# Which weights and values stay on chip, in which places, and in which pieces the query weights come

## The chip, the cores and the metric

The kernel runs on one core of a Trainium2 chip. The core has five engines that run side by side: TensorE (PE, matrix products, with its weight loads PEld), VectorE (DVE), ScalarE (ACT), GpSimd (POOL) and SyncE (SP), which here only issues DMA transfers. Transfers bring data from HBM to the on-chip memory SBUF; TensorE writes its results to PSUM, which has eight banks. The metric is the device time in microseconds (us) of one execution; lower is better.

## The reference

Two rounds of attention and a gated feed-forward block (GLU) for 4 batch rows with one new token each. Both rounds use the same caches and weights.

```python
def _A_ref(x, k_cache, v_cache, wq, wo):
    W = min(4096, max(256, Sk // 4))          # 2048 of 8192 positions
    q = (x @ wq).reshape(B, Sq, Hq, Dh)...    # 32 query heads of 128
    k = jnp.repeat(k_cache[:, :, Sk - W:, :], rep, axis=1)   # 8 key heads, rep = 4
    v = jnp.repeat(v_cache[:, :, Sk - W:, :], rep, axis=1)
    p = softmax(q k^T * Dh ** -0.5)
    return (p v).reshape(B, Sq, Hq * Dh) @ wo
def _B_ref(x, w_gate, w_up, w_down):          # 512 -> 1792 -> 512
    return (sigmoid(x @ w_gate) * (x @ w_up)) @ w_down
x = x + _A_ref(_layernorm(x), ...)
x = x + _B_ref(_layernorm(x), ...)
x = x + _A_ref(_layernorm(x), ...)
x = x + _B_ref(_layernorm(x), ...)
```

All inputs are bf16. The keys of the window are 16 MB, the values 16 MB, the query weights 4 MB, the output weights 4 MB, and gate, up and down weights 1.75 MB each.

## The kernel before

**Order of the work.** The kernel records every operation with its reads, writes and PSUM banks in a list; a planner (`_schedule`) then orders the list for each engine by estimated times, and `_assign_sync` adds the waits on semaphores. All transfers but one go through SP, in the order in which they are recorded. A transfer waits until the place that it fills has been read for the last time, and everything behind it on SP waits with it. Line L464 is the one line that issues them.

**Layers.** The code counts four layers: 0 is attention, 1 the GLU, 2 attention again, 3 the GLU again. In layer 0 each of 8 heads loads its keys (2 MB), turns them with TensorE (L740) and keeps the turned keys in `kt` for layer 2. Scores are made at L763, the softmax maximum at L772 to L782, the exponential at L785, the weights are turned at L796 and spread at L821 (VectorE) and L828 (ScalarE). Values are loaded (`load_v`, 2 MB a head) and multiplied at L863 or L921; where several blocks are summed in one product, ScalarE copies the partial sums at L872 and TensorE adds them at L879. The output weights are applied at L988 or L946 and L895. In layer 2 the keys are there already, and values, and the weights that are not kept, are loaded again.

**Places.** SBUF is cut into units of 256 columns, 64 KB over all 128 partitions. `ar` is an arena of 75 units, `sx` a side area of 31, `ws` the output weights' place (64 units), `kt` the keys' place (256), `pt`, `pb` and `qs` small buffers. A dictionary `WHERE` says which units a load fills, and `blk_tok` turns units into tokens through which the planner finds who must have read them. Between layers 0 and 2 the output weights of five blocks of `ws` are moved aside into PSUM banks (`stash`, L1036) and brought back by ScalarE (L1031), so that their units can hold feed-forward and query weights.

**What is kept before.** Rows 0 and 1 of gate and up (`u01`, `g01`, 28 units) are loaded in layer 1 and used again in layer 3. Of the values, 8 units of head 0 and 13 units of head 7 stay from layer 0 to layer 2 (`VKEEP` names the piece that `load_v` leaves out). Together these are 49 units. Half of the query weights stays too (`WKEEP`); the other half (32 units) is streamed again for layer 2, as three pieces listed in `WHERE["q01"]`.

**The stretch around the change.** After the last head of layer 0, layer 1's weights come: up rows 0 and 1, gate rows 0 and 1, gate rows 2 and 3, up rows 2 and 3, then the down weights in six pieces. `glu` runs its products at L1157 in the order up 0, up 1, gate 0 to 3, up 2, up 3, and the down products at L1233 (L1230 in layer 3). Then the streamed query weights, then values for layer 2. `project_q` multiplies the query weights (L703), takes the mean off (L716) and scales by the reciprocal deviation (L719), which GpSimd makes at L634; heads 0 to 3 and 4 to 7 of the keys have a half of `qs` each (tokens `qs` and `qs1`). The first scores of layer 2 wait for the first half alone, the later ones for both. `scores` alternates between the PSUM banks in `SB2 = [3, 0]`; the bank `MB` (4) takes a part of the turned weights later. A memset of `qs` by GpSimd (L1318) runs before the queries are written, because a weight piece has lain there.

## Time and profile before

| | us |
|---|---|
| median of 3 runs (lowest, highest) | 174.04 (173.87, 174.45) |
| the profiled execution | 174.79 |
| its span, first to last instruction | 173.0 |
| TensorE busy | 136.2 |
| VectorE busy | 100.7 |
| ScalarE busy | 77.3 |
| transfers, moved | 68.93 MB, 398 GB/s over the span |

The profiled execution is one of its own and not among the three of the median. In the profile a line such as `L863 PE MATMUL ps<-kt,pt` is an operation of TensorE at line 863 that writes `ps` and reads `kt` and `pt`; what stands in brackets is the time that its engine sat idle before and who ended it. `SPq` is the issue of a transfer, and the time of landing is given apart. The granted TensorE clock (PEclk) is a share of full speed.

### The profile page before, as it was taken

How to read it: one execution, taken by the hardware profiler on the slowest of the kernel's cores; microseconds unless marked ns; L12 is line 12 of the kernel's file. 1: busy time of each engine (PE TensorE's matmuls, PEld its weight loads, DVE VectorE, ACT ScalarE, POOL GpSimd, SP SyncE). 2: the span in 40 equal slices, each digit the busy share in tenths (PEclk: the TensorE clock that was granted, in tenths of full speed). 3: DMA queues.
4: the chain of work that ended last, by engine and by line, in shares of the span. 5: the costliest groups of instructions: out<-in, count | busy, mean ns of one | idle time of the engine just before them, and what ended most of it. 6: DMA issues, size and time to landing. Idle time of an engine off the chain costs nothing.

```text
span 173.0 us, 4894 instructions
## 1 busy us (share of the span) xinstructions
PE 136.2 (79%) x2179; PEld 100.4 (58%) x2179; DVE 100.7 (58%) x252; ACT 77.3 (45%) x134; POOL 8.0 (5%) x19
## 2 busy tenths in 40 slices
PE   0395589899898779998979676657977989689883
PEld 0292388658466458565655366546625756458772
DVE  7535015886848675795797653113279877754450
ACT  2064207848576646566291230110767463554200
POOL 5200000000000000000000000202200000000020
PEclk9999756999999987999999755555569999956755
DMA  5999999999999999999999999999999999999960
GB/s 183 424 422 411 432 424 428 439 409 449 424 416 433 400 445 424 412 427 428 420 417 418 397 419 416 406 400 411 386 385 452 426 420 405 424 416 423 407 250 5
DMA packets 9361, 68.93 MB, mean 398 GB/s; under 512 B 1017, under 2 KB 1917, under 8 KB 6013
## 3 DMA queue, kind: packets, MB, share of 16 engines
q1 hardware_dynamic: 9332, 68.62, 95.7%
q8 instruction: 17, 0.28, 0.6%
q14 instruction: 4, 0.02, 0.0%
q10 hardware_dynamic: 8, 0.00, 0.0%
HBM read 68.62 MB, written 0.00 MB: 397 GB/s over the span
## 4 chain that ended last, share of the span: by engine, by line
DMA 65%; PE 23%; DVE 6%; ACT 2%; issue 2%; SPq 1%; DVEq 0%; ACTq 0%
DMA arena<-in_A_v_cache_dram 32%; DMA kt<-in_A_k_cache_dram 12%; DMA kt<-in_A_v_cache_dram 10%; DMA wo_sb<-in_B_w_down_dram 7%; PE ps L863 5%; PE ps L740 4%; DMA wo_sb<-in_A_wq_dram 4%; PE ps L763 3%; PE ps L1157 2%; PE ps L921 2%; SPq L464 1%; DVE pt L821 1%; PE ps L1230 1%; PE ps L836 1%; PE ps L988 1%
## 5 line engine op out<-in xcount | busy, mean ns | idle before, releaser
L750 ACT COPY kt<-ps 128x1024 bf16<-128x1024 bf16 x40 | 39.2, 1017 | 28.2 <-PE ps L740 28.0
L740 PE MATMUL ps<-ident_r,kt 128*128 128x128 bf16 x512 | 40.4, 238 | 5.1 <-DMA kt<-in_A_k_cache_dram 3.1
L740 PEld LDWEIGHTS ps<-ident_r,kt 128*128 128x128 bf16 x512 | 34.9, 109 | 11.8 <-issue 4.4
L750 DVE COPY kt<-ps 128x1024 bf16<-128x1024 bf16 x24 | 29.1, 1214 | 14.2 <-PE ps L740 14.0
L763 PE MATMUL ps<-kt,qs 128*32 128x512 bf16 x256 | 18.3, 413 | 1.2 <-ACT pb L785 1.2
L821 DVE TENSOR_TENSOR pt<-ps,ofbr 128x1024 bf16<-128x1024 f32 (+1 forms) x15 | 15.4, 1029 | 2.7 <-PE ps L796 2.7
L863 PE MATMUL ps<-arena,pt 128*64 128x512 bf16 (+1 forms) x128 | 13.1, 377 | 3.0 <-DMA arena<-in_A_v_cache_dram 3.0
L772 DVE TENSOR_REDUCE nmz<-ps 128x1 f32<-128x512 f32 x16 | 11.0, 688 | 5.9 <-PE ps L763 5.8
L791 DVE STREAM_TRANSPOSE pb<-pb 128x512 bf16<-128x512 bf16 x16 | 11.3, 704 | 4.2 <-ACT pb L785 4.1
L785 ACT ACTIVATE pb<-ps,nmz 128x512 bf16<-128x512 f32 x16 | 11.1, 692 | 5.8 <-DVE nmz L782 5.8
L828 ACT ACTIVATE pt<-ps,ofbr 128x96 bf16<-128x96 f32 x28 | 7.2, 342 | 7.8 <-PE ps L796 7.8
L863 PEld LDWEIGHTS ps<-arena,pt 128*64 128x64 bf16 (+1 forms) x128 | 5.9, 111 | 7.9 <-DMA arena<-in_A_v_cache_dram 4.0
L763 PEld LDWEIGHTS ps<-kt,qs 128*32 128x32 bf16 x256 | 5.8, 101 | 7.8 <-ACT pb L785 2.2
L872 ACT COPY arena<-ps 128x512 f32<-128x512 f32 (+1 forms) x7 | 3.9, 555 | 11.9 <-PE ps L863 11.7
L1031 ACT COPY wo_sb<-ps 128x1024 bf16<-128x1024 bf16 x5 | 5.0, 1011 | 9.1 <-PE ps L703 9.1
L836 PE MATMUL ps<-rowf,nmz 128*128 128x16 f32 x32 | 6.9, 292 | 2.7 <-DVE pt L821 2.5
L836 PEld LDWEIGHTS ps<-rowf,nmz 128*128 128x128 f32 x32 | 5.4, 212 | 5.8 <-DVE pt L821 4.2
L1157 PE MATMUL ps<-xn,arena 128*128 128x5 bf16 (+1 forms) x168 | 6.3, 172 | 2.2 <-DMA arena<-in_B_w_up_dram 1.1
L634 POOL TENSOR_TENSOR rs<-pt,rs 128x4 f32<-128x4 f32 x3 | 3.0, 1014 | 106.0 <-DVE pt L630 106.0
L879 PEld LDWEIGHTS ps<-arena 128*128 128x128 f32 x52 | 6.7, 201 | 2.1 <-ACT arena L872 1.6
L879 PE MATMUL ps<-arena 128*128 128x16 f32 x52 | 7.4, 273 | 0.6
L1157 PEld LDWEIGHTS ps<-xn,arena 128*128 128x128 bf16 x168 | 6.3, 118 | 2.5 <-DMA arena<-in_B_w_up_dram 1.2
(170 smaller groups left out, 162.9 us busy)
## 6 DMA issues: line engine op xcount, KB each, us to landing
kt<-in_A_k_cache_dram SPq DMA_DIRECT2D x8, 2048.0 KB, 24.6
arena<-in_A_v_cache_dram SPq DMA_DIRECT2D x7, 2048.0 KB, 20.2
kt<-in_A_v_cache_dram SPq DMA_DIRECT2D x3, 2048.0 KB, 14.9
wo_sb<-in_A_wo_dram SPq DMA_DIRECT2D x8, 512.0 KB, 25.1
kt<-in_A_v_cache_dram SPq DMA_DIRECT2D x4, 1024.0 KB, 19.3
kt<-in_A_wq_dram SPq DMA_DIRECT2D x1, 2048.0 KB, 11.7
side<-in_A_wq_dram SPq DMA_DIRECT2D x1, 1984.0 KB, 15.8
arena<-in_B_w_up_dram SPq DMA_DIRECT2D x2, 896.0 KB, 8.0
```

What stands on the lines that cost most here:

```text
L740: last = pe.transpose(bankb(bank)[:, (v * NB + q) * 128:(v * NB + q + 1) * 128], kt[:, c0:c0 + 128], ident_b[:, :])
L750: return (e.tensor_copy if ev == "vector" else e.copy)(to, fr)
L763: last = pe.matmul(ps[32 * b:32 * b + 32, sbk, 0:CB * 128], qs[:, q0:q0 + 32], blk_ap(kblk(h, b))[:, c * CB * 128:(c + 1) * CB * 128], sta ...
L772: lambda v: v.tensor_reduce(nmv, ps[:, sbk, 0:CB * 128], AXX, ALU.max, negate=True),
L785: o = a.activation(pbuf[:, :], ps[:, sbk, 0:CB * 128], ACTF.Exp, bias=gv, scale=1.0, accum_out=zv)
L791: P.op("vector", "ptr%d_%d" % (L, h), 650.0, lambda v: v.transpose(turned[:, :], pbuf[:, :]), r=[("pb", 0), ("pb", 1)], w=[("pb", 2), ("pb ...
L821: lambda v: v.tensor_tensor(pv4[:, 0:nj], spread(tbk, nj).unsqueeze(2).broadcast_to([128, nj, NB, REP]), ofb[:, :].unsqueeze(1).unsqueeze( ...
L828: last = a.mul(pv4[:, nj:NJ4, b, :], spread(MB, NJ4 - nj), ofb[:, b:b + 1])
L836: lambda pe: pe.matmul(ps[:, tbk, CB * NQ:CB * NQ + NR], zv.broadcast_to([128, 128]), rowf[:, :], start=True, stop=True),
L863: last = pe.matmul(ps[rows * g:rows * (g + 1), bank, 0:wide * 128].rearrange("p (c d) -> p c d", c=wide), ptv[:, w0:w0 + rows], v, start=( ...
L879: last = pe.matmul(ps[:, out[0], out[1]:out[1] + NR], part[:, c * 128:(c + 1) * 128], ey[wide][:, c * NR:(c + 1) * NR], start=(c == 0), st ...
L1157: last = pe.matmul(ps[:, bank, fc * wid:(fc + 1) * wid], cols[:, fc - g0, :], xn[:, ktc * (NB + 1):ktc * (NB + 1) + wid], start=(ktc == 0 ...
```

## The change

**Kept.** Gate rows 0 are no longer kept; up rows 0 and 1 and gate rows 1 are (21 units). Of the values 24 units of head 0 and 15 of head 7 are kept. Together 60 units. In layer 3, gate rows 0 are loaded again (7 units, into `kt`, free by then).

**Places and pieces.** The kept weights and values change places, and the rest is fitted around them. In layer 1 up rows 2 and 3 come as 7 units, 4 units and 3 units, in `ar`, `pb` and `qs`; gate rows 2 and 3 come before 0 and 1. The down weights come in the order of blocks 4 to 5, 0 to 3, 8 to 11, 6 to 7, 12 to 13, partly in places that layer 1's own gate rows have just left. The streamed query weights come in five pieces of 8, 8, 8, 4 and 4 units instead of three of 10, 14 and 8, and not in row order: the first two hold both halves of the rows for the first sixteen query heads, which serve key heads 0 to 3. They go to places that layer 1's weights leave. Value head 0 of layer 2 needs one load instead of four.

**Scores.** The first scores of layer 2 are made in bank `MB` instead of bank 3.

**Order in the feed-forward.** A variable `turn` gives the order of the products: up 0, up 1, then gate 2, 3, 0, 1 in layer 1 and gate 1, 0, 2, 3 in layer 3, then up 2, up 3. Which product opens and closes an accumulation follows from it.

```diff
-    KEEPG = 4
+    KEPTG = {("u", 0), ("u", 1), ("g", 1)}
...
-    VKEEP = {0: 24, 7: 19}
+    VKEEP = {0: 8, 7: 17}
...
-        WHERE["V0_%d" % (HKV - 1)] = [ar(0, 19), ar(23, 13)]
-        WHERE["u01"], WHERE["g01"] = ar(52, 2 * GU), ar(38, 2 * GU)
+        WHERE["V0_%d" % (HKV - 1)] = [ar(15, 17), ar(0, 15)]
+        WHERE["u01"], WHERE["g01"] = ar(36, 2 * GU), ar(22, 2 * GU)
...
-            "g23_1": ("ws", 8, 2 * GU), "u23_1": ar(0, 2 * GU),
-            "d0_1": ar(14, 8), "d4_1": ("ws", 22, 6), "d7_1": ar(36, 2), "d8_1": ("qs", 0, 4), "d10_1": ("pb", 0, 4),
-            "d12_1": ("pt", 4, 4),
-            "q01": [("ws", 8, 10), ar(0, 14), ("ws", 18, 8)],
-            "V2_0": [ar(14, 9), ar(36, 2), sx(0, 8), sx(8, 5), ar(66, 8)],
-            "V2_1": [sx(13, NS - 13), ar(0, 14)],
+            "g23_1": ("ws", 8, 2 * GU), "u2_1": ar(15, GU), "u3_1": ("pb", 0, 4), "u3_1b": ("qs", 0, 3),
+            "d4_1": ("ws", 24, 4), "d6_1": ("pt", 4, 4), "d0_1": ("ws", 8, 8), "d8_1": ("ws", 16, 8), "d12_1": ar(25, 4),
+            "q01": [(0, ar(15, 8)), (16, ("ws", 8, 8)), (8, ("ws", 16, 8)), (24, ("ws", 24, 4)), (28, ar(25, 4))],
+            "V2_0": [sx(0, 8), ar(50, 24)],
+            "V2_1": [sx(8, NS - 8), ar(15, 9)],
             "V2_6": [("kt", 128, 16), ("kt", 144, 16)],
-            "V2_7": [("kt", 160, 12), ("kt", 172, 7), ar(23, 13)],
-            "g23_3": ar(0, 2 * GU), "u23_3": sx(0, 2 * GU),
-            "d0_3": ar(14, 8), "d4_3": ("kt", 192, 8), "d8_3": ("kt", 200, 8), "d12_3": sx(14, 4),
+            "V2_7": [("kt", 160, 10), ("kt", 170, 7), ar(0, 15)],
+            "g0_3": ("kt", 0, GU), "g23_3": ar(15, 2 * GU), "u23_3": sx(0, 2 * GU),
+            "d0_3": ("kt", 8, 8), "d4_3": ("kt", 192, 8), "d8_3": ("kt", 200, 8), "d12_3": sx(14, 4),
...
+        def qz(s):
+            return (("qs",), ("qs1",)) * (s[0] == "qs")
+
+        def load_g(L, nm, ktc):
+            kept = (nm, ktc) in KEPTG
+            name = "%s%d_%d" % (nm, ktc, L)
+            if not kept and name in WHERE:
+                got, f0 = [], 0
+                for x in (name, name + "b"):
+                    if x in WHERE:
+                        s, c0 = WHERE[x], ktc % 2 * F + f0 * 128
+                        dma("w" + x, blk_ap(s), (wg_d if nm == "g" else wu_d)[:, ktc // 2, c0:c0 + s[2] * UNIT], w=blk_tok(s) + qz(s),
+                            rate="bw_4k")
+                        got.append((s, f0))
+                        f0 += 2 * s[2]
+                return got
...
-            for nm, ktc in (("u", 0), ("u", 1), ("g", 0), ("g", 1), ("g", 2), ("g", 3), ("u", 2), ("u", 3)):
+            turn = [("u", 0), ("u", 1)] + [("g", a) for a in ((1, 0, 2, 3) if last_layer else (2, 3, 0, 1))] + [("u", 2), ("u", 3)]
+            for at, (nm, ktc) in enumerate(turn):
...
-                parts[1:] = [(4, 7), (7, 8), (8, 10), (10, 12), (12, 14)]
+                parts = [(4, 6), (0, 4), (8, 12), (6, 8), (12, 14)]
...
-        for w in WHERE["q01"]:
+        for u0, w in WHERE["q01"]:
...
-            turns.append(scores(2, n, h, SB2[n % 2], TB2[n % 2]))
+            turns.append(scores(2, n, h, SB2[n % 2] if n else MB, TB2[n % 2]))
```

In `VKEEP` the number is the unit at which the kept piece starts within the head, so `0: 8` means that head 0's units from 8 on are kept. In `q01` the number is the unit at which a piece starts; units 0 to 15 are the first rows of each pair of row blocks, 16 to 31 the second.

More of the change, by code (lines that the diff above doesn't have):

```diff
@@ L421, in build @@
         MAIN = WKEEP[2][0][1]
-        G0 = MAIN - KEEPG * GU
         def ar(u, n):
@@ L1040, in build @@
         gkeep = {}
-        def load_g(L, nm, ktc, keep):
-            key = (nm, ktc // 2, 0 if keep or (nm, ktc // 2, 0) in gkeep else L)
+        def qz(s):
[13 more added lines that the diff above has]
+                return got
+            key = "%s%d%d" % (nm, ktc // 2 * 2, ktc // 2 * 2 + 1) + ("" if ktc < 2 else "_%d" % L)
+            s = WHERE[key]
             if key not in gkeep:
-                s = WHERE["%s%d%d" % (nm, key[1] * 2, key[1] * 2 + 1) + ("_%d" % L if key[2] else "")]
                 gkeep[key] = s
-                dma("w%s%d_%d" % (nm, L, ktc), blk_ap(s), (wg_d if nm == "g" else wu_d)[:, key[1], :], w=blk_tok(s),
-                    rate="bw_7k")
-            s = gkeep[key]
-            return (s[0], s[1] + ktc % 2 * GU, GU)
+                dma("w" + key, blk_ap(s), (wg_d if nm == "g" else wu_d)[:, ktc // 2, :], w=blk_tok(s), rate="bw_7k")
+            return [((s[0], s[1] + ktc % 2 * GU, GU), 0)]
         def load_d(L, fc0, fc1):
@@ L1056, in load_d @@
             dma("wd%d_%d" % (L, fc0), blk_ap(s)[:, 0:(fc1 - fc0) * D], rows[:, (fc0 - g0) * D:(fc1 - g0) * D],
-                w=blk_tok(s) + (("qs",), ("qs1",)) * (s[0] == "qs"), rate="bw_4k")
+                w=blk_tok(s), rate="bw_4k")
             return s
@@ L1146, in glu, with e_g @@
             wid = NB if last_layer else NB + 1
-            for nm, ktc in (("u", 0), ("u", 1), ("g", 0), ("g", 1), ("g", 2), ("g", 3), ("u", 2), ("u", 3)):
+            turn = [("u", 0), ("u", 1)] + [("g", a) for a in ((1, 0, 2, 3) if last_layer else (2, 3, 0, 1))] + [("u", 2), ("u", 3)]
+            for at, (nm, ktc) in enumerate(turn):
                 bank = GB if nm == "g" else UB
-                keep = not last_layer and 2 * ktc + (nm == "u") < KEEPG
-                s = load_g(L, nm, ktc, keep)
-                def e_g(pe, ktc=ktc, s=s, bank=bank):
+                first, end = ktc == turn[0 if nm == "u" else 2][1], ktc == turn[-1 if nm == "u" else 5][1]
+                got = load_g(L, nm, ktc)
+                def e_g(pe, ktc=ktc, got=got, bank=bank, first=first, end=end):
                     last = None
@@ L1155, in e_g @@
                         g0, gn = WD[fc // 4]
-                        cols = blk_ap(s)[:, g0 * 128:(g0 + gn) * 128].rearrange("p (m j) -> p j m", j=gn)
+                        s, f0 = [x for x in got if x[1] <= fc][-1]
+                        cols = blk_ap(s)[:, (g0 - f0) * 128:(g0 - f0 + gn) * 128].rearrange("p (m j) -> p j m", j=gn)
                         last = pe.matmul(ps[:, bank, fc * wid:(fc + 1) * wid],
@@ L1159, in e_g @@
                                          xn[:, ktc * (NB + 1):ktc * (NB + 1) + wid],
-                                         start=(ktc == 0 and fc == 0), stop=(ktc == NC - 1),
-                                         skip_group_check=True)
+                                         start=(first and fc == 0), stop=end, skip_group_check=True)
                     return last
                 prev = [P.op("tensor", "glu_%s%d_%d" % (nm, L, ktc), 36.0 * NFC, e_g,
-                             r=list(blk_tok(s)) + [("xn",)], w=[("psg", bank, ktc)], banks=(bank,), order=prev)]
+                             r=[t for s, _ in got for t in blk_tok(s)] + [("xn",)], w=[("psg", bank, ktc)], banks=(bank,), order=prev)]
                 toks[nm].append(("psg", bank, ktc))
@@ L1233, in e_d @@
                                 last = pe.matmul(ps[:, YB, c * NB:(c + 1) * NB], wd, hf,
-                                                 start=(fc == 0 and c == 0), stop=(fc == NFC - 1),
+                                                 start=(fc == parts[0][0] and c == 0), stop=(fc == parts[-1][1] - 1),
                                                  skip_group_check=True)
@@ L1315, in build @@
         glu(1, False)
-        P.op("gpsimd", "qs_zero", 1200.0, lambda g: g.memset(qs[:], 0.0), w=[("qs",), ("qs1",)] + list(blk_tok(WHERE["d8_1"])))
+        P.op("gpsimd", "qs_zero", 1200.0, lambda g: g.memset(qs[:], 0.0), w=[("qs",), ("qs1",)] + list(blk_tok(WHERE["u3_1b"])))
         layer_norm(2, SCALE)
         streamed = []
-        u0 = 0
-        for w in WHERE["q01"]:
+        for u0, w in WHERE["q01"]:
             dma("wq2_%d" % u0, blk_ap(w), wq_d[:, 0, u0 * UNIT:(u0 + w[2]) * UNIT], w=blk_tok(w),
@@ L1329, in build @@
                     streamed.append((blk_ap(t), blk_tok(t), ktc, q0, q1))
-            u0 += w[2]
-        assert u0 == HQ
+        assert sum(w[2] for _, w in WHERE["q01"]) == HQ
         project_q(2, kept_q + streamed, 1)
```

## The prediction

> **What bounds the kernel now.** I read the page's slices and its chain of waits first, then the windows of busy time, the DMA issues of the stretch 98 to 132 us with their time to landing, and the timeline around the places the change touches.
>
> ```profile
> GB/s 183 424 422 411 432 424 428 439 409 449 424 416 433 400 445 424 412 427 428 420 417 418 397 419 416 406 400 411 386 385 452 426 420 405 424 416 423 407 250 5
> DMA 65%; PE 23%; DVE 6%; ACT 2%; issue 2%; SPq 1%; DVEq 0%; ACTq 0%
> ```
>
> The transfers run near 420 GB/s in every slice but the first and the last two, and 65% of the chain is transfers. So bytes count, as long as nobody lets the queue run dry.
>
> ```profile
> core 0: us, PE busy (x) PEld busy (x) DVE busy (x) ACT busy (x) POOL busy (x), PEclk, DMA share, GB/s
> 98.90:112.40 13.50, 9.42 (x191) 8.05 (x190) 4.77 (x17) 2.96 (x5) 1.01 (x1) 0.50 1.01 414
> 118.40:123.40 5.00, 4.30 (x125) 4.01 (x125) 2.16 (x12) 1.09 (x2) 1.35 (x3) 0.50 1.01 395
> 123.40:127.10 3.70, 3.64 (x48) 1.60 (x48) 1.85 (x6) 2.86 (x3) 0.00 (x0) 0.50 1.01 378
> 132.60:142.50 9.90, 9.39 (x226) 6.81 (x223) 8.47 (x25) 6.08 (x23) 0.00 (x0) 1.00 1.00 425
> ```
>
> The last two columns say that even where the rate falls to 378 GB/s the DMA share is full: the loss there is small pieces, not an empty queue.
>
> ```profile
> wo_sb<-in_A_wq_dram SPq DMA_DIRECT2D x1, 512.0 KB, 6.9
> arena<-in_A_v_cache_dram SPq DMA_DIRECT2D x1, 576.0 KB, 8.0
> side<-in_A_v_cache_dram SPq DMA_DIRECT2D x1, 512.0 KB, 6.7
> side<-in_A_v_cache_dram SPq DMA_DIRECT2D x1, 320.0 KB, 6.9
> ```
>
> Issue time plus the last column is a landing. The last q piece lands at 116.54 + 6.9 = 123.4, the pieces of value head 0 at 116.91 + 8.0 = 124.9, then (issued 119.68) 126.4 and (120.25) 127.2.
>
> ```profile
> 98.89 0.34 SPq L464 DMA_DIRECT2D arena<-in_B_w_up_dram  x1
> 103.39 0.33 SPq L464 DMA_DIRECT2D arena<-in_B_w_up_dram  x1
> 116.54 0.33 SPq L464 DMA_DIRECT2D wo_sb<-in_A_wq_dram  x1
> 121.93 1.01 POOL L634 TENSOR_TENSOR rs<-pt,rs 128x4 f32<-128x4 f32 x1 [1.29 <-DVE pt L630]
> 123.46 0.59 PE L703 MATMUL ps<-xn,wo_sb 128*128 128x4 bf16 x16 [0.36 <-DMA wo_sb<-in_A_wq_dram]
> 123.98 3.60 PE L763 MATMUL ps<-kt,qs 128*32 128x512 bf16 x32
> 142.57 1.06 PE L863 MATMUL ps<-kt,pt 128*32 128x256 bf16 x32 [0.36 <-DMA kt<-in_A_v_cache_dram]
> 147.49 1.06 PE L863 MATMUL ps<-kt,pt 128*32 128x256 bf16 x32 [0.35 <-DMA kt<-in_A_v_cache_dram]
> 149.99 0.62 PE L863 MATMUL ps<-kt,pt 128*32 128x256 bf16 x16 [0.90 <-DMA kt<-in_A_v_cache_dram]
> 168.09 0.48 PE L1230 MATMUL ps<-arena,pt 128*25 128x128 bf16 x9 [0.35 <-DVE pt L1201]
> 169.09 0.40 PE L1230 MATMUL ps<-arena,pt 128*25 128x128 bf16 x7 [0.52 <-issue]
> 170.03 0.53 PE L1230 MATMUL ps<-side,pt 128*25 128x128 bf16 x8
> ```
>
> The brackets show what PE waited for: the last q piece before the second layer's first scores, value heads 3, 4 and 5, and the activations before the last products. The last transfer (issued 150.28, 18.8 to landing) lands at 169.1, the last product ends at 170.56. Transfers and computation run neck and neck over the last 30 us; both must come forward for the end to move.
>
> **The transfers, part by part.** A unit is 64 KB.
> Value head 0 keeps 24 units instead of 8, so four pieces become one of 512 KB. They took 127.2 - 123.4 = 3.8 us; the 512 KB piece took 126.4 less the 125.1 of the piece before it (issued 117.5, 7.6), 1.3. Gain 2.5.
> Value head 7 keeps 15 instead of 13: 128 KB at 420 GB/s, gain 0.3.
> Gate rows 0 are no longer kept and are loaded again for the last feed-forward block: 448 KB, half of an 896 KB load, which lands 164.7 - 162.6 = 2.1 after the one before it (issued 143.51 and 142.88, 21.2 and 19.7). Loss 1.05.
> Smaller pieces: 256 KB pieces land 0.65 to 0.7 apart (117.0, 117.7, 118.4), 0.17 per unit, against 0.157 for an 896 KB load in 2.2. Pieces of up to 256 KB hold 27 units after and 14 before (value head 0 apart): 13 x 0.015 = 0.2 lost. The split of head 1 into 23 and 9 units instead of 18 and 14 moves the same bytes; its 5.3 us against 5.0 at 420 GB/s leave between 0 and 0.3 to win. I take 0.1.
> Sum: 2.5 + 0.3 + 0.1 - 1.05 - 0.2 = 1.65 us, close to the byte count (11 units, 0.72 MB, 1.7 us at 420). The last load lands at about 167.4. By the time value head 2 loads, the gain is 2.4; there lies the room for PE.
>
> The Trainium skill, "DMA: Bandwidth & Descriptors", section "Bandwidth", speaks against the split: it wants at least 1 MiB in a transfer and gives 341 GB/s at 1 MB. This trace disagrees for queued pieces, which at 256 KB in 0.7 us still make 375 GB/s. At the page's rate 27 units would take 5.2 us where I count 4.6, so the sum would be 1.0 and not 1.65.
>
> **The waits that the new places add.** SP issues in order, so a late one holds all behind it. How long an empty queue needs from issue to first data isn't in this stretch. Bounds: the 4 KB output comes back 1.05 after its issue; the very first 2 MB load lands 7.6 after issue, 5.0 of them data, 2.6.
> Up rows 0 and 1 now lie where the sums of head 0 stand, and wait for L879 (100.39) instead of the values' products (98.89). The queue holds values until 103.6 (95.3 plus 8.3, the same bytes in front after); the load would land at 100.4 + 2.6 + 2.2 = 105.2 at worst, before the 105.8 of now. Cost 0.
> Gate rows 0 and 1 wait for the first piece of head 7's products (103.39), behind gate rows 2 and 3, which fill the queue to 108. Cost 0.
> The first 4-row down piece waits for the products with gate rows 2 and 3: these land at 108.0, PE has done up rows 1 by 108.8, 28 products take 1.0 (42 took 1.49), issue 109.8. In front of it the queue holds up rows 0 and 1 (landing 105.8), gate rows 2 and 3 (108.0), 0 and 1 (110.2), 448 KB (111.3) and three small pieces (1.75 us), to 113. Cost 0, and 0.6 at most if the products slip 1 us.
> The second q piece waits until that down piece is used: landing 115.8 (all down pieces by 106.15 + 12.2 = 118.4 as now, less 1.25 and twice 0.65 for the three behind it), 16 products 0.59, issue 116.5. With 1.22 of data and 2.6 it lands by 120.3; in line, behind 118.4 and 1.25 for the first, it lands at 120.9. Cost 0, cover only 0.6. The third (down piece 8 to 12) stands 0.6 better. Behind them wait all value loads; this is the thinnest place.
> GpSimd's memset of qs waits for the last up products, about 113.2, instead of 117.5; not needed before 122.9. Cost 0.
>
> **The computation.** The first query half is complete with q pieces one and two (120.9), not 123.4, so its scaling waits for GpSimd's L634, ending 122.94: evacuation to 123.27. PE meanwhile takes the third q piece. The first scores start at 123.3 instead of 124.0: gain 0.7. Standing in bank MB, they free the third scores from waiting for the first exponential (0.70 and 1.61 of idle on PE and PEld at 128.28); yet PEclk is 0.50 there, and at that clock they take 1.8 and not 1.07, and the softmax steps keep DVE's order, so I count 0.5 to 0.7 for all of it. Then PE's waits for values (0.36 + 0.35 + 0.90 = 1.6) go, since those land 2.4 earlier. That is 2.1 to 2.3 at most; one score more lands between heads 4 and 5 in the new order, which may eat some. I take 2.0 at the last layer's start; bounds 0.7 (the softmax chain fills the waits) and 2.4 (all that transfers allow). The feed-forward at the end keeps its 5.8 us from L1071 to the first L1230 and 2.5 behind it. Moving gate row 1 to the front and one down piece to kt issues nothing on that path: all these loads land before their use.
>
> End by transfers: 167.4 + 0.53 for the last 8 products = 167.9, by computation 170.56 - 2.0 = 168.6. The later sets it: 2.0 us gained, span 171.0. The profiled execution was 174.79 (span 173.0 and 1.8 around it), 0.75 above the median of 174.04; taken from the median this is 172.0 us.
>
> **Rivals.**
> First, the softmax chain of the second layer keeps its pace: PE's waits for values turn into waits for DVE and ACT (DVE is busy 8.47 of 9.90 us at 132.6). Then only the earlier first scores remain, 0.7 to 1.0: about 173.2. Against it: each of three heads showed a real transfer wait.
> Second, nothing: the scores find no earlier start because the q pieces come later in their small parts, and the last-layer loads, with 448 KB more, end level with now. 174.0. Against it: the sum of the transfers.
> Third, slower: SP's chain of reused places lets the queue run dry. The place is the second q piece behind the first big down piece; each microsecond that the up products and with them the activations are late beyond 0.5 is lost once for every byte behind. It decides from about 0.5 + 1.65 = 2.2 us late, or from three such places 1.2 late each, since each refills only what lies before it. At 3 us late, about 175.0. For it: before, q pieces of 1.5 MB were issued ahead of that point, now 0.5 MB. Against it: 112.4 us for the last up rows in both orders.
>
> Fourth, each added piece pays a fixed price. Four more pieces under 700 KB are issued; from the rows a 256 KB piece costs 0.7 against 0.62 at 420 GB/s, so 0.08 each, 0.3 in all, 172.3 and inside the forecast's range. Three times that price would give 173.0. The rule of the Trainium skill's "DMA: Bandwidth & Descriptors", section "Bandwidth", is the one that points this way, and the 375 GB/s speak against it.
>
> **How the numbers follow.** Forecast 0.60 (its own range 171.2 to 172.9); softmax pace 0.12; pieces dearer than counted 0.03; nothing 0.08; dry queue 0.17. The changes under 0.3% (0.5 us), about what a measurement of this kernel can tell from none, are the second rival's. So faster 0.75, same 0.08, slower 0.17. Range 171.0 to 174.5: it leaves out most of the dry queue and a small tail below, where the 0.52 of idle at 169.09 would go too.
>
> **What would show it.** Right: 0.7 MB less on the DMA queue, last down load near 167.4, first scores near 123.3, no or shorter waits for values on PE. Wrong: slices under 380 GB/s with a DMA share under 1 between 112 and 125; PE waiting on down pieces or q pieces for longer than now; the second layer's value products no earlier than before although the values are there; a longer stretch from the last values to the end.

## The result, and the profile after

The kernel after the change takes 175.81 us, the median of six runs (175.17 to 176.72), beside 174.08 us for the kernel before in six runs on the same chip (173.87 to 174.47). The ratio is 1.0102, with a 95% interval from 1.0079 to 1.0125: the change costs 1.0%, where 172.0 us was forecast. The profiled execution took 175.39 us, its span 173.6 us. The spans of the two profiled executions differ by 0.6 us only, the medians by 1.7: the profile of before stands 0.7 us above its median and that of after 0.4 below. So the profiles below show where time goes, and the sizes are taken from the timed runs.

The page of the changed kernel, its rate in 40 slices and its chain of waits:

```profile
GB/s 182 423 424 418 422 430 436 428 402 442 423 412 429 415 438 427 413 430 428 428 414 409 398 324 395 393 357 318 291 431 438 428 427 408 423 420 409 416 352 12
DMA 63%; PE 24%; DVE 5%; ACT 2%; issue 2%; SPq 2%; DVEq 0%; ACTq 0%
```

Slice 24 (about 100 to 104 us) and slices 27 to 29 (113 to 126 us) fall to 291 to 357 GB/s; before, no slice between the first and the last two was under 385. The windows of the same stretch (stretch, length, busy time of the engines, granted clock, DMA share, GB/s):

```profile
core 0: us, PE busy (x) PEld busy (x) DVE busy (x) ACT busy (x) POOL busy (x), PEclk, DMA share, GB/s
98.90:112.40 13.50, 9.97 (x201) 8.21 (x194) 4.51 (x15) 2.24 (x3) 1.01 (x1) 0.50 0.97 374
112.40:118.40 6.00, 3.07 (x79) 2.62 (x77) 0.81 (x5) 1.53 (x2) 0.97 (x1) 0.50 1.03 366
118.40:123.40 5.00, 4.14 (x117) 3.80 (x117) 2.08 (x12) 0.14 (x1) 1.00 (x2) 0.50 0.84 273
```

The second of these windows before, which the prediction does not show:

```profile
112.40:118.40 6.00, 3.04 (x76) 2.63 (x76) 0.51 (x3) 0.81 (x1) 0.82 (x1) 0.50 1.05 405
```

The DMA share, the last figure but one, was 1.01 in the third window before and is 0.84 now: the transfer engines are idle part of the time. In the second window it stays full, at 1.03, although the rate fell by 39 GB/s, so the share alone does not show an empty queue there. Against the rates before (414, 405, 395) these windows moved 40 x 13.5 + 39 x 6 + 122 x 5 = 1384 KB less, 3.3 us at 420 GB/s. All saved bytes together were worth 1.65 us. The issues, with KB and us from issue to landing:

```profile
wo_sb<-in_B_w_down_dram SPq DMA_DIRECT2D x2, 512.0 KB, 6.1
wo_sb<-in_A_wq_dram SPq DMA_DIRECT2D x2, 512.0 KB, 5.5
arena<-in_B_w_up_dram SPq DMA_DIRECT2D x1, 896.0 KB, 5.6
side<-in_A_v_cache_dram SPq DMA_DIRECT2D x1, 512.0 KB, 7.3
side<-in_A_v_cache_dram SPq DMA_DIRECT2D x1, 1472.0 KB, 9.5
```

And the timeline at the places of the prediction (start, length, engine and line; in brackets the idle time before and what ended it):

```profile
101.27 0.34 SPq L462 DMA_DIRECT2D arena<-in_B_w_up_dram  x1
106.11 5.48 SPq L462 DMA_DIRECT2D wo_sb<-in_B_w_down_dram  x3
117.10 2.11 SPq L462 DMA_DIRECT2D wo_sb<-in_A_wq_dram  x3
120.35 1.85 SPq L462 DMA_DIRECT2D side<-in_A_v_cache_dram  x2
124.17 0.59 PE L701 MATMUL ps<-xn,wo_sb 128*128 128x4 bf16 x16 [0.94 <-DMA wo_sb<-in_A_wq_dram]
124.69 1.90 PE L761 MATMUL ps<-kt,qs 128*32 128x512 bf16 x16
147.42 1.06 PE L861 MATMUL ps<-kt,pt 128*32 128x256 bf16 x32 [0.71 <-DMA kt<-in_A_v_cache_dram]
157.51 1.03 PE L919 MATMUL ps<-pt,kt 128*128 128x32 bf16 x32 [0.41 <-DMA kt<-in_A_v_cache_dram]
163.53 1.00 PE L1170 MATMUL ps<-xn,arena 128*128 128x4 bf16 x26 [0.85 <-issue]
168.69 0.48 PE L1242 MATMUL ps<-kt,pt 128*25 128x128 bf16 x9 [0.36 <-DVE pt L1213]
```

Read beside the prediction's steps (landings are issue plus time to landing, from the trace):

| | forecast | after |
|---|---|---|
| up rows 0 and 1 issued, landed | 100.4, by 105.2 | 101.27, 106.8 |
| first four-row down piece issued, landed | 109.8, 115.8 | 110.79, 116.4 |
| second query piece issued, landed | 116.5, 120.9 | 117.10, 122.4 |
| first scores of layer 2 | 123.3 | 124.69 |
| value head 2 landed (before: 137.5) | 135.1 | 137.4 |
| last down piece landed | 167.4 | 170.5 |
| layer 3's activations to its first down product | 5.8 | 6.5 |

### The profile page after: what moved, and what is told of

It reads as the page before. It is cut to its first block, busy times and chain, and to the rows that moved or that the text cites. A ratio compares the mean times of both kernels' runs of the same rounds, so it can differ in the third digit from the quotient of the medians.

```text
span 173.6 us, 4895 instructions
## 1 busy us (share of the span) xinstructions
PE 133.4 (77%) x2179; PEld 98.3 (57%) x2179; DVE 100.7 (58%) x252; ACT 77.1 (44%) x134; POOL 8.0 (5%) x19
## 2 busy tenths in 40 slices
DMA packets 9504, 68.21 MB, mean 393 GB/s; under 512 B 1032, under 2 KB 1804, under 8 KB 6156
## 4 chain that ended last, share of the span: by engine, by line
DMA 63%; PE 24%; DVE 5%; ACT 2%; issue 2%; SPq 2%; DVEq 0%; ACTq 0%
DMA arena<-in_A_v_cache_dram 32%; DMA kt<-in_A_k_cache_dram 13%; DMA kt<-in_A_v_cache_dram 12%; PE ps L861 4%; DMA wo_sb<-in_B_w_down_dram 4%; PE ps L738 4%; PE ps L1170 3%; PE ps L761 3%; DMA wo_sb<-in_A_wq_dram 3%; PE ps L919 3%; SPq L462 2%; PE ps L1242 1%; ACT pb L783 1%; DVE nmz L770 1%; PE ps L794 1%
## 5 line engine op out<-in xcount | busy, mean ns | idle before, releaser
L738 PE MATMUL ps<-ident_r,kt 128*128 128x128 bf16 x512 | 38.8, 232 | 5.9 <-DMA kt<-in_A_k_cache_dram 3.8
L738 PEld LDWEIGHTS ps<-ident_r,kt 128*128 128x128 bf16 x512 | 33.1, 106 | 12.9 <-DMA kt<-in_A_k_cache_dram 4.2
L1170 PE MATMUL ps<-xn,arena 128*128 128x5 bf16 (+1 forms) x140 | 5.7, 173 | 2.7 <-DMA arena<-in_B_w_gate_dram 0.9
L1170 PEld LDWEIGHTS ps<-xn,arena 128*128 128x128 bf16 x140 | 5.5, 118 | 3.1 <-issue 1.6
```

Source lines behind the costliest of these rows:

```text
L738: last = pe.transpose(bankb(bank)[:, (v * NB + q) * 128:(v * NB + q + 1) * 128], kt[:, c0:c0 + 128], ident_b[:, :])
L1170: last = pe.matmul(ps[:, bank, fc * wid:(fc + 1) * wid], cols[:, fc - g0, :], xn[:, ktc * (NB + 1):ktc * (NB + 1) + wid], start=(first and ...
```

## The experiments

All times are medians beside runs of the kernel before on the same chip; the ratio is to those.

| run | us | ratio, 95% interval |
|---|---|---|
| the changed kernel | 175.81 | 1.0102 (1.0079 to 1.0125) |
| x0_control | 175.80 | 1.0104 (1.0056 to 1.0152) |
| x1_q_free | 175.01 | 1.0047 (1.0028 to 1.0067) |
| x2_up_free | 175.40 | 1.0072 (1.0046 to 1.0099) |
| x3_up_down_free | 174.82 | 1.0042 (1.0011 to 1.0073) |
| y1_gate_first | 175.30 | 1.0056 (1.0037 to 1.0075) |
| z1_before_bank | 174.31 | 1.0002 (0.9973 to 1.0031) |
| z2_before_half | 174.51 | 1.0021 (0.9993 to 1.0049) |
| x6_all_free | 173.00 | 0.9935 (0.9914 to 0.9955) |
| x5_v_free | 175.80 | 1.0097 (1.0066 to 1.0128) |
| x7_all_but_v | 174.92 | 1.0053 (1.0024 to 1.0082) |
| g1_kept_first | 174.79 | 1.0048 (1.0018 to 1.0078) |
| r3_no_reload | 174.78 | 1.0030 (1.0003 to 1.0056) |
| b1_gate_kept_first | 174.37 | 1.0005 (0.9982 to 1.0029) |
| o1_before_kept_last | 174.88 | 1.0027 (1.0004 to 1.0050) |
| s1_before_reload | 174.65 | 1.0028 (1.0010 to 1.0045) |
| t1_all_three | 173.94 | 0.9989 (0.9962 to 1.0017) |
| c2_keep16 | 175.87 | 1.0098 (1.0063 to 1.0133) |
| c3_keep12 | 176.49 | 1.0130 (1.0098 to 1.0162) |

The medians of the kernel before beside these runs lay between 174.04 and 174.32, so a difference of two rows in us can be wrong by up to 0.3; the ratios are free of this.

### Places that are free early

To take a load's wait away without a race it needs a place that nobody reads late. The key arena gives one, if in layer 2 a head is scored against another head's keys: the output is then another, the amount of work the same.

```diff
-                                         blk_ap(kblk(h, b))[:, c * CB * 128:(c + 1) * CB * 128],
+                                         blk_ap(kblk(HKV - 1 if L and h == HKV - 2 else h, b))[:, c * CB * 128:(c + 1) * CB * 128],
```

The control has this edit alone. 

> The changed kernel, except that in the second layer head 6 is scored against the keys of head 7, so that the 32 units of the key arena that held head 6's keys are free after the first layer (its output is not the reference's; amount of work and of transfers as in the changed kernel). It is the base for the next three. All theories expect the time of the changed kernel, 175.8 us, within 0.4, and the same dips of the transfer rate at 101 to 104 us and at 118 to 126 us.

The three others move loads into the 32 units so freed.

```diff
-            "q01": [(0, ar(15, 8)), (16, ("ws", 8, 8)), (8, ("ws", 16, 8)), (24, ("ws", 24, 4)), (28, ar(25, 4))],
+            "q01": [(0, ("kt", 192, 8)), (16, ("kt", 200, 8)), (8, ("kt", 208, 8)), (24, ("kt", 216, 4)), (28, ("kt", 220, 4))],
```

> As the control (head 6 scored against head 7's keys), with the five query pieces, of the same sizes and in the same order, in the freed units, so that none waits for the products with a down piece. Theory (the queue runs dry where a load waits for the last reader of its place): pieces two and three are issued about 113.3 instead of 117.1 and 118.4, the dip at 118 to 125 us goes, and the time falls by 1.2 to 2.0 us against the control, to about 174. Rival 1 (pieces of 256 and 128 KB with 2 KB rows are slow by themselves): the dip stays although they are issued early, and the time falls by less than 0.4. Rival 2 (PE's order: the third piece stands before the first scores): the scores come no earlier than the third piece, which comes earlier only if the queue is the cause. Rival 3 (the reloaded gate row and the loads of the last block): no change.

```diff
-        WHERE["u01"], WHERE["g01"] = ar(36, 2 * GU), ar(22, 2 * GU)
+        WHERE["u01"], WHERE["g01"] = ("kt", 208, 2 * GU), ar(22, 2 * GU)
```

> As the control (head 6 scored against head 7's keys), with up rows 0 and 1 in freed units, so that their load waits neither for the values' products nor for the sums of head 0. Theory: the load is issued as early as the values before it (about 95), the dip at 101 to 104 us goes, everything behind it lands 0.5 to 1.0 us earlier, until the down and query pieces, whose issue depends on the computation; the dip at 118 to 125 us stays or grows smaller by what comes earlier. Time 0.3 to 1.0 us less than the control. Rivals 1, 2 and 3: no change.

The last has that edit and another:

```diff
-            ... "d0_1": ("ws", 8, 8), "d8_1": ("ws", 16, 8), ...
+            ... "d0_1": ("kt", 192, 8), "d8_1": ("kt", 200, 8), ...
```

> As the control (head 6 scored against head 7's keys), with up rows 0 and 1 and the two four-row down pieces in freed units: the load of the up rows, the two down pieces and the two query pieces that followed them in their places (they keep those places, free since the products with gate rows 2 and 3) wait for nothing late. Theory: both dips go, transfers come 2.5 to 3.3 us earlier from 126 us on, and the time falls by 2 to 3 us against the control, to 172.8 to 173.8, below the kernel before (174.0). Rivals 1 and 3: the rate stays low at 118 to 125 us, or the gain is lost at the end, and less than 0.5 us is won. Rival 2: the scores come earlier only with the third query piece, by up to 1 us, and the end by as much.

The control is the changed kernel's equal. The edits won 0.8, 0.4 and 1.0 us, each at the low end of what was expected or below it, and none reaches the kernel before. The intervals of the first and the third lie below that of the changed kernel (1.0079 to 1.0125), so these waits are real; the 0.4 us of the up rows alone lies within the intervals. With the query pieces freed, the third window moved 377 GB/s at a share of 1.04. With the up rows and the down pieces freed, the windows read

```profile
98.90:112.40 13.50, 9.69 (x204) 8.45 (x204) 4.46 (x17) 2.73 (x4) 1.01 (x1) 0.50 1.02 410
112.40:118.40 6.00, 2.51 (x62) 2.12 (x62) 0.52 (x3) 0.67 (x1) 0.98 (x1) 0.50 1.03 402
118.40:123.40 5.00, 4.43 (x137) 4.18 (x138) 2.43 (x13) 0.71 (x1) 1.21 (x2) 0.50 0.82 296
123.40:127.10 3.70, 3.70 (x40) 1.34 (x44) 1.64 (x6) 3.24 (x4) 0.00 (x0) 0.50 0.86 298
```

The first two windows are whole again; the hole has moved to 118 to 127 us. Something else is late there. The trace names it: value head 0's 8 units are issued at 119.77 and value head 1's first 23 at 121.08, because their place `sx` holds kept query weights, which are read only by layer 2's query products, after the last down product. Before, the same place was filled at 119.68 to 120.99; but 11 units of value head 0 had been sent into the arena at 116.91 and 117.50, and bridged the time. These 11 are among the 16 that the change saves. That is the second theory; the first was that the up rows, down pieces and query pieces are issued late.

### The parts alone, on the kernel before and in another order

The changed kernel with the gate load recorded first:

```diff
+            if not last_layer:
+                load_g(L, "g", 2)
             for at, (nm, ktc) in enumerate(turn):
```

> The changed kernel with one edit: the load of gate rows 2 and 3, whose place is free early, is issued before the load of up rows 0 and 1, which waits for the sums of head 0; the products keep their order. Theory: the dip at 101 to 104 us goes (the gate load fills the queue meanwhile), the up rows land 1 to 1.5 us later than in the changed kernel and their products with them, the gate products no later; the dip at 118 to 126 us stays. 0 to 0.6 us faster than the changed kernel, 175.2 to 175.8. If the dry stretch at 101 us cost its whole 0.9 us, it would be 174.9. Rivals: no change.

The kernel before with the bank:

```diff
-            turns.append(scores(2, n, h, SB2[n % 2], TB2[n % 2]))
+            turns.append(scores(2, n, h, SB2[n % 2] if n else MB, TB2[n % 2]))
```

> The kernel before with only the first scores of the second layer in bank MB. Theory: no cost, a gain of 0 to 0.3 us: 173.8 to 174.1. Rival 2 (the bank hurts: the transposed weights of head 0 and the tail of the scores share MB, and the second scores start no earlier): slower by 0.3 to 1.0 us, 174.4 to 175.1.

And with the bank and the half rows:

```diff
-            "q01": [("ws", 8, 10), ar(0, 14), ("ws", 18, 8)],
+            "q01": [(0, ("ws", 8, 8)), (16, ar(0, 8)), (24, ar(8, 6)), (30, ("ws", 16, 2)), (8, ("ws", 18, 8))],
...
-        for w in WHERE["q01"]:
+        for u0, w in WHERE["q01"]:
```

> The kernel before, with the first scores in bank MB and the streamed query weights by half rows, first heads first, in five pieces (8, 8, 6, 2 and 8 units) in the places that they had; nothing else of the change. Theory: pieces that are queued early cost nothing by themselves; the first half of the queries is complete some 1 us earlier and the time is 173.6 to 174.1. Rival 1: the small pieces with 1 to 4 KB rows are slow, the rate falls below 380 GB/s from 115 to 123 us, and the time is 174.6 or more.

The first fills the hole at 101 us (404 GB/s from 98.9 to 112.4, share 1.00) and wins 0.5 us; its interval, too, lies below that of the changed kernel. The bank shows no cost (1.0002). The time with the half rows, 174.51, lies between what was expected (up to 174.1) and their rival (174.6 or more), and its interval reaches from no cost to 0.5%. Two of their windows keep a full share:

```profile
112.40:118.40 6.00, 3.13 (x80) 2.74 (x81) 0.52 (x3) 1.10 (x1) 0.95 (x1) 0.50 1.03 388
118.40:123.40 5.00, 4.31 (x129) 3.95 (x132) 2.43 (x13) 1.34 (x2) 1.23 (x3) 0.50 1.02 376
```

They move less than before (388 for 405 GB/s, 376 for 395), and the next window more (428 for 378), so that over the three the bytes are level. So the pieces and the bank are not what makes the change slow by 1.0%; a cost of the pieces of up to half of that is not excluded.

### The values behind the query weights

With heads 4, 5 and 6 scored against head 7's keys, 96 units are free. One run frees everything, one the values alone, one everything but the values:

```diff
-            "V2_0": [sx(0, 8), ar(50, 24)],
-            "V2_1": [sx(8, NS - 8), ar(15, 9)],
+            "V2_0": [("kt", 151, 8), ar(50, 24)],
+            "V2_1": [("kt", 128, 23), ar(15, 9)],
```

The first has, beside this, the edits of the up rows and down pieces above, and `q01` as `[(0, ("kt", 160, 8)), (16, ("ws", 8, 8)), (8, ("ws", 16, 8)), (24, ("kt", 172, 4)), (28, ("kt", 168, 4))]`. 

> As the changed kernel, but in the second layer heads 4, 5 and 6 are scored against head 7's keys (amount of work as before), so that 96 units of the key arena are free after the first layer. There lie now: up rows 0 and 1, the two four-row down pieces, three of the five query pieces, value head 0's 8 loaded units and value head 1's first 23. So no load between 95 and 126 us waits for a late reader but the second quarter of value head 1 and the query pieces' own order. Theory 2, formed from the run in which only the up rows and down pieces were freed (its value head 2 landed at 137.37, as in the kernel before, 137.47, although the reused places no longer held anything up): value head 1's first piece was issued at 121.08 there, because its place holds kept query weights that are read only after the second layer's normalization (before: 120.99 for the same bytes), and its data began some 3.3 us later, while the queue in front of it had run out; the 16 units saved of value head 0 lie before that point and so win nothing. It expects value head 2 to land 1.0 to 1.8 us earlier than 137.4 (then its own place, head 0's keys, scored until 125.3, is the next bound), and the time at 173.0 to 174.0. Rival 1 (small pieces are slow by themselves): value head 2 at 137.0 to 137.4, time 174.6 to 175. Rival 3 (the reloaded gate row and the tail): value head 2 earlier, but the time stays at 174.6 to 175.

The second has the two lines alone. 

> The changed kernel with heads 4, 5 and 6 of the second layer scored against head 7's keys, and only value head 0's 8 loaded units and value head 1's first 23 in freed places; the up rows, down pieces and query pieces lie as in the changed kernel. Value heads 0 and 1 are then issued right behind the last query piece (119.5) and not at 120.35 and 121.66. Theory 2 alone (the wait for the kept query weights is the cause): 0.8 to 1.3 us faster, 174.5 to 175.0. Theory 1 alone (the query pieces' late issue, 117.1 and 118.4, is the cause and the values are only behind them): at most 0.3 faster, 175.5 to 175.8. Both in line: value heads 0 and 1 come 0.3 to 0.6 earlier, and all of it is won only if the query pieces come early too, as in the run with everything freed (173.0).

The third has the rest without them. 

> The run with everything freed (173.0), but with value heads 0 and 1 in the changed kernel's places, where they wait for the kept query weights (heads 4, 5 and 6 scored against head 7's keys). Theory 2 (that wait uncovers once nothing else does, because the 16 units saved of value head 0 no longer fill the queue): value head 2 lands 0.9 to 1.6 us later than in that run (135.4), at 136.3 to 137.0, and the time is 174.0 to 174.6. If the places of the values do not matter: 173.0 to 173.3.

Everything freed takes 173.0 us, 0.65% less than before; the values alone win nothing (175.8); everything but the values wins 0.9 (174.92). The two waits stand in series on one queue: 0 and 0.9 us singly, 2.8 together. That heads 4 to 6 use other keys wins nothing by itself, since the second run has this too. The windows from 118.4 us on, first with everything freed but the values, then with everything:

```profile
118.40:123.40 5.00, 4.56 (x137) 4.27 (x141) 2.42 (x13) 0.86 (x1) 1.21 (x2) 0.50 0.93 346
123.40:127.10 3.70, 3.70 (x44) 1.27 (x40) 1.63 (x6) 3.17 (x5) 0.00 (x0) 0.50 0.91 339
```

```profile
118.40:123.40 5.00, 4.35 (x133) 4.17 (x133) 2.62 (x14) 0.54 (x1) 1.20 (x2) 0.50 1.07 427
123.40:127.10 3.70, 3.70 (x46) 1.42 (x47) 1.59 (x7) 3.41 (x4) 0.00 (x0) 0.50 1.01 404
```

81 x 5 + 65 x 3.7 = 646 KB, 1.5 us at 420 GB/s, of the 1.9 by which the medians differ. The time of the third run (174.92) is 0.3 above what the theory allowed. Its profiled execution (173.73) was the fastest of its eleven and shows the hole in the rates, yet value head 2 landed at 135.1 there, where 136.3 to 137.0 was expected, and in the run with everything freed at 135.4. So the 1.9 us rest on the medians of eleven runs each; how the hole reaches the end of the kernel, the trace does not show.

The run with the values alone shows that late issues are not the whole of the hole either:

```profile
119.26 2.10 SPq L462 DMA_DIRECT2D kt<-in_A_v_cache_dram  x2
118.40:123.40 5.00, 3.77 (x109) 3.51 (x109) 2.70 (x14) 0.73 (x1) 1.20 (x2) 0.50 0.75 232
122.00:124.50 2.50, 0.63 (x24) 0.54 (x21) 0.49 (x2) 1.80 (x2) 1.01 (x1) 0.50 0.87 220
```

The query pieces and the first loads of value heads 0 and 1 were all issued by 119.93. From 122.0 to 124.5 some 2.2 to 2.7 MB issued over 2 us earlier stood in the queue, and it moved 220 GB/s. Value head 0 landed at 129.1, for 127.6 after the change, and not 0.3 to 0.6 us earlier as expected. In the changed kernel, too, the rate was 176 GB/s from 122.5 to 124.0, with 0.9 MB or more issued over 2 us before. So once late issues have let the queue run low, it moves slowly for some us even with loads in it; why is open.

### The tail

Neither theory touches the 0.85 us for which PE stands idle up to 163.53. One edit of the changed kernel takes back PE's order, one leaves out the load of gate rows 0 (the kept gate rows 1 stand in for them, so the output is another); then both kinds of edit on the kernel before. The first:

```diff
-            for s, j0 in () if wide else pieces:
+            for i_, (s, j0) in enumerate(() if wide else pieces):
+                if L and n == HKV - 1 and i_ == 0:
+                    prev = early7
+                    continue
+                if L and n == HKV - 2 and i_ == 1:
...
+                    prev = [P.op("tensor", "PV%d_%d_%d" % (L, HEADS2[n + 1], j7), ...)]   # head 7's kept values
```

> The changed kernel, with one edit of PE's order: in the second layer the 30 products of value head 7 with its kept values stand between head 6's two pieces, as the 26 did in the kernel before, and not behind them. Seven profiles of kernels with the change's places show PE idle for 0.85 to 1.42 us with nothing that the profile names, after the first two gate and up products of the last feed-forward block; three profiles with the old places show 0 to 0.24 there. Each time a fetch of 16 KB (the instruction queue) begins about 1.8 us after PE passes the same instruction in the former, and 1.3 in the latter, and PE goes on about 2.6 us after the fetch began. Theory 3 (PE waits there for its own instructions, because after the change more products stand between the last wait for values and the first gate and up products): the idle time falls to 0.3 or less and the time by 0.5 to 0.8 us, to 175.0 to 175.3. Rival: the idle time belongs to the loads (the weights, the reloaded gate row); then it stays, and the time with it, 175.8.

With the gate rows first too: 

> The changed kernel with two edits together: gate rows 2 and 3 loaded before up rows 0 and 1 (175.3 alone), and the products with head 7's kept values between head 6's pieces. If both act and add up, 174.4 to 174.8; if the second does nothing, 175.3.

Without the load of gate rows 0:

```diff
+            if name == "g0_3":
+                return [(("ar", 29, GU), 0)]
             if not kept and name in WHERE:
```

> The changed kernel without the load of gate row 0 in the last feed-forward block: its products there use the kept gate row 1 in its place (the output is not the reference's, PE's work is the same). 448 KB less. Theory: the last down piece lands 1.05 us earlier (169.4 for 170.5), but the end is set by PE, so 0 to 0.3 us faster, 175.5 to 175.8. Rival 3 (the reload is what costs): 1.0 us faster, 174.8.

The kernel before with the order of after:

```diff
+            if L and n == HKV - 1:
+                prev = list(prev) + [o for o in P.ops if o.name == "sel2_%d" % HEADS2[n - 1]]
             for s, j0 in () if wide else pieces:
```

> The kernel before, with one edit of PE's order: in the second layer the 26 products of value head 7 with its kept values stand behind head 6's (the order of the changed kernel's last part), nothing else. If the order is what the run with head 7's kept products put first won 1.0 us by, this loses as much: 174.7 to 175.3, with 0.5 to 0.9 us of idle time of PE after the first two gate and up products. If the order costs nothing with the old loads: 174.0 to 174.4.

The kernel before with the reload:

```diff
         def load_g(L, nm, ktc, keep):
+            if (L, nm, ktc) == (3, "g", 0):
+                s = ("kt", 0, GU)
+                dma("wg0_3", blk_ap(s), wg_d[:, 0, 0:F], w=blk_tok(s), rate="bw_4k")
+                return s
```

> The kernel before, with gate row 0 loaded again for the last feed-forward block (448 KB into a free place, ahead of gate rows 2 and 3, as in the changed kernel); nothing else. If the reload alone costs what leaving it out of the changed kernel won (1.0 us): 174.9 to 175.4. If it hides behind the computation with the old loads: 174.0 to 174.5; the last down piece lands 1.05 us later, at 170.1, where PE uses it at 170.0 to 170.6.

And three edits of the changed kernel together (gate rows first, kept values first, no reload): 

> The changed kernel with three edits together: gate rows 2 and 3 loaded before up rows 0 and 1 (0.5 us alone), head 7's kept products first (1.0 alone), and no load of gate row 0 in the last block (1.0 alone; gate row 1 stands in for it, so the output is not the reference's). If the three add up: 173.2 to 173.6, faster than the kernel before. If reload and order are one cost (PE's idle time in the tail) seen twice: 174.0 to 174.4.

Order and reload each won 1.0 us in the changed kernel, the reload as its rival said and not as expected; in the kernel before they cost 0.7 and 0.5 us. The kernel before shows 0.24 us of idle time at this place, and with the other order alone 0.98:

```profile
162.93 1.00 PE L1157 MATMUL ps<-xn,arena 128*128 128x4 bf16 x26 [0.24 <-issue]
```

```profile
161.81 0.23 PE L1159 MATMUL ps<-xn,arena 128*128 128x4 bf16 x2 [0.27 <-DVE xn L1073]
163.02 0.99 PE L1159 MATMUL ps<-xn,arena 128*128 128x4 bf16 x26 [0.98 <-issue]
```

So the order makes this wait, with the old loads. The step from 0.24 to 0.98 is of the size of the loss, 0.7. In the other direction the idle time fell only to 0.66 us, not to 0.3 as expected, and 1.0 us was won all the same: there the order acts by more than this wait, and by what stays open. With the reload, the kernel before waits for a down piece near its end:

```profile
161.75 1.07 PE L1161 MATMUL ps<-xn,arena 128*128 128x4 bf16 x28 [0.27 <-DVE xn L1075]
169.18 0.61 PE L1234 MATMUL ps<-kt,pt 128*25 128x128 bf16 x16 [0.53 <-DMA kt<-in_B_w_down_dram]
```

The kernel before sits idle at this place for as long without a named cause (0.52 us, at 169.09 in the prediction's lines), so the 0.5 us of loss can't be read from this line. What it shows is that the transfers now set the end: the last two down pieces land at 169.13 and 169.75 and are used at 169.18 and 169.79. In the changed kernel without the reload, PE's idle time at the first place was 0.36 and not 0.85. The three edits together won 1.9 us, not the 2.5 of the single ones, so they overlap. The gate order and the kept values alone are additive (0.5 + 1.0, and 1.4 together) and bring the changed kernel level with the one before, with everything computed: 1.0005.

### Kept units given back as free places

If free places were what lacked, a version between the two should win. Both versions have the gate order and the kept values first; the first of them:

```diff
-    VKEEP = {0: 8, 7: 17}
+    VKEEP = {0: 16, 7: 17}
...
-            "q01": [(0, ar(15, 8)), (16, ("ws", 8, 8)), (8, ("ws", 16, 8)), (24, ("ws", 24, 4)), (28, ar(25, 4))],
-            "V2_0": [sx(0, 8), ar(50, 24)],
-            "V2_1": [sx(8, NS - 8), ar(15, 9)],
+            "q01": [(0, ar(15, 8)), (16, ar(50, 8)), (24, ("ws", 24, 4)), (8, ("ws", 8, 8)), (28, ar(25, 4))],
+            "V2_0": [sx(0, 16), ar(58, 16)],
+            "V2_1": [sx(16, NS - 16), ar(15, 9), ar(50, 8)],
```

> A version without any alias: the changed kernel with 52 kept units in place of 60 (16 of value head 0 in place of 24), where the 8 units set free take the second query piece, which then waits for nothing late; the fourth query piece stands before the third, which lies in the place of the first four-row down piece; gate rows 2 and 3 first, and head 7's kept products first (these two together gave 174.37). 512 KB more to load than the changed kernel, 192 KB less than before. If a place that is free early is worth as much as the kept unit that it displaces: the query pieces come about 1 us earlier, value head 0 is 8 units (1.26 us) longer, and the time is 174.0 to 174.4. If the dry stretch cost more than the units saved: below 174.0. If kept units are worth more: 174.8 or more.

> The same with 48 kept units (12 of value head 0): the fifth query piece has a free place too, so that after the first down pieces no query piece but the third waits for a late reader. 256 KB more than the version with 52; 64 KB more than before. If free places are worth more than kept units until the queue stays full: 173.8 to 174.2. If the trade is even: as the version with 52, within 0.3. Else slower by up to 0.6.

Both are slower, 175.87 and 176.49. The query pieces did come early (the last landed at 123.6, for 126.4 after the change), but value head 0 could still not be issued before 120.0, and it was 8 and 12 units longer. 174.37 (60 units kept) + 8 x 0.157 = 175.6, and + 12 x 0.157 = 176.3: the added units are paid in full, and the early query pieces give nothing back. This reading was formed after the runs. It agrees with the second theory: what is sent before the wait for the kept query weights is free, what stands behind it counts.

## Why the prediction was wrong, by its own steps

**What bounds the kernel** was read rightly, with its condition: bytes count as long as the queue does not run dry. That the 378 GB/s from 123.4 to 127.1 came of small pieces does not hold: with the same pieces, the kernel before with the bank alone moved 414 there.

**The transfers.** The bytes are right (68.93 to 68.21 MB), and so is the size as a potential: with all places free the kernel beats the one before by 1.1 us, in spite of the tail. But 2.5 us were booked for value head 0 as if all its units lay on the path. 11 of the 16 saved units, 1.7 us, had been sent while SP waited for the kept query weights anyway. The chance that smaller pieces cost more did not show on the kernel before, beyond an interval that allows 0.5%.

**The waits that the new places add** is the step that failed. Every wait stood there at cost 0. The four that were named had the right readers, and were issued 0.6 to 1.0 us later than computed, of which some 0.5 is this execution's (the last load of values landed at 104.13, for 103.64 before); they cost 1.0 us (up rows and down pieces freed). The last up rows, for which 112.4 was counted in both orders, landed at 113.94. The cover was the error: it was counted to the landing of the piece in front, with 2.6 us for an empty queue. A landing is the last of a transfer's sixteen signals; in the trace of before those of the 896 KB of up rows came from 103.85 to 105.82 us, so a sixteenth of the queue is empty 2 us ahead of the landing, and the other parts follow. A piece that comes late shows it:

```profile
side<-in_A_v_cache_dram SPq DMA_DIRECT2D x1, 512.0 KB, 5.2
```

This is value head 0 in the run with everything but the values freed: issued at 119.62, first signal at 122.78, last at 124.86. 512 KB are 1.25 us at 420 GB/s, so 1.9 us (to the first signal) to 4.0 us (to the landing) go elsewhere. The piece in front gave its first signal at 120.18 and its last at 123.39. If each part keeps its order, the fastest part had thus run dry for some 1.3 us and the slowest hardly at all: the landing is late mostly because that part still had work, while others stood empty. "Cover only 0.6" for the second query piece, counted to a landing, was no cover: it landed at 122.4, 2.1 us behind the first, for 1.25 of data. The sentence "Behind them wait all value loads" was true and stopped one step short: the values have a wait of their own, for the kept query weights, and which of the removed bytes had covered it was not asked. That wait is worth 1.9 us (174.92 against 173.00) where the others are gone, and nothing where they stand (175.8).

**The computation.** The first scores came at 124.69 and not at 123.3, because the third query piece, landed at 124.1, stands ahead of them in PE's order; the prediction let PE take it while it waited. PE's waits for values did not go: 0.71 and 0.41 us remain in the lines above and 0.31 at 152.39, since value head 2 lands as late as before. "The feed-forward at the end keeps its 5.8 us" is 6.5 in the profile. The diff does not write PE's order, but the planner moved head 7's kept products behind head 6's, and that alone costs the kernel before 0.7 us. And "all these loads land before their use" held by a hair: the last down piece lands at 170.46 and is used at 170.63; in the kernel before the reload costs 0.5 us.

**The rivals.** The third, the dry queue, is in the main what happened, at the place that it named and at two more; 175.0, which it gave for 3 us late, is 0.8 below the result, and the tail, which no rival named, is of that size. The second, that nothing comes of it, describes the values: level with before at 137.4. The fourth, dearer pieces, finds no support in the half rows on the kernel before, whose interval allows up to 0.5%. The first was not put to the test. The upper end of the range, 174.5, left most of the third rival out, and held none of the tail's 1 us.

## What to carry to other kernels

In this kernel a byte saved was worth time only behind the last wait of the transfer queue; what was sent while the queue's issuer waited anyway was free, and was cover. Before a place is reused, list for each load its last reader, and ask what fills the queue until 2 us after its issue, counted to the first signal of the piece in front and not to its landing; keeping more on chip can take away just the places that would fill it. Where a planner sets the order, compare the engines' orders too, and not only the diff.

## What the runs showed of the hardware

The sixteen parts of a queue drift apart. Value head 2's signals came over 3.0 us before (134.43 to 137.47) and over 1.7 us after (135.75 to 137.42). That the late issues let the slow parts catch up, so that 3.3 us of lost transfer time cost less than 3.3 us, is argued; with the up rows and down pieces freed, the spread was 1.9 us at value head 0 and 3.0 again at value head 2. A piece issued into a queue that runs dry gave its first signal 1.9 us later than its data alone explain. The Trainium skill, "DMA: Bandwidth & Descriptors", section "Anatomy of one DMA — SWDGE (gpsimd) path", gives about 2.0 us as fixed, for another way of issue. By the first signal the trace agrees (1.9); the landing, at 4.0, holds the wait of the slow parts behind the piece in front as well.

PE can wait in a row of products for nothing that the profile names. In all profiles with the new places it stood idle after the second gate and up product of the last block, from 0.36 us (no reload) to 1.42 us (everything freed), and a 16 KB fetch on the instruction queue had begun 2.4 to 2.6 us before it went on. At the next such place after the change, 0.52 us up to 169.69, the fetch had begun at 167.14, 2.55 us before. The Trainium skill, "Runtime: NRT & Kernel Launch", section "Instruction fetch mechanics", says that code comes in blocks of 16 KB by the sequencer's own transfers and that crossing a block is mostly hidden. Here it is not hidden where PE runs a long stretch without another wait, if the fetch is indeed the cause: that it is was argued from the times only. That PE's order decides the wait is shown; why leaving out a load of 448 KB shortens it too is open.
